# Batch 2's K and Q brought in and cast earlier, and the opening reordered, in a sliding-window attention and feed-forward kernel

## The chip, the cores and the metric

The kernel runs on one core of a Trainium2 chip. The time is device microseconds of one execution. Lower is better. The runs of the kernel before are summarised by their median.

## The reference

Eight batches of eight heads, 576 positions, head size 64. Each query sees itself and the 63 positions before it. The heads' outputs are put side by side and go through a feed-forward block with a product of two projections.

```python
scores = (1 / sqrt(64)) * q @ k.T
scores = where((rel >= 0) & (rel < 64), scores, -1e9)   # rel = query position - key position
attn   = softmax(scores)
x      = (attn @ v) as [8 * 576, 512]                   # heads side by side
out    = ((x @ w1) * (x @ w2)) @ w3 @ w_out             # w1, w2: 512x1024; w3: 1024x1024; w_out: 1024x512
```

All inputs and the output are float32.

## The kernel before

The kernel keeps everything in fp16 on the core and accumulates in fp32. Its order is written out by hand: each engine executes its instructions in the order in which the Python code issues them, and waits only for the data and buffers that the next instruction needs. TensorE is PE, VectorE is DVE, ScalarE is ACT, GpSimd is POOL, and SP only issues transfers.

*Attention.* A batch's K and Q come as float32 rows into a tile `stage` (three buffers, 1.18 MB each, two transfers for the even and the odd heads, L210). `cast_qk` (L226) turns each half into fp16 in `k16` or `q16`, of which there is one buffer each. `transposes` (L262, copies L266) turns them into `kT` and `qT`, 18 PE transposes in three groups of six, through banks of the accumulation memory. V normally arrives already in its place `v16` by transfers with a cast on the way (`load_v`, L241, issued by POOL); `copy_v` (L245) fills overlapping blocks on DVE. Batch 0's V is the exception: it comes as rows, is cast, transposed (`transposes(0, "v", ...)`) and transposed back by `keys_of_v` (L273, L275).

`scores(d)` (L296) makes the scores of one half of a third of a batch, so a batch has six: 0 to 5 are batch 0, 6 to 11 are batch 1. ACT takes the exponentials into `pt` (L300, six buffers), and POOL cuts the window out of it with two selects per piece (L308, L310). The scores share a single bank pair `s_ps`, so the next `scores` waits for the exponential of the last. `values(d)` multiplies by V (L338 in batches 0 and 1, L354 later), ACT forms the reciprocal of the sums as exp(-ln) (L344, L345; later L360 to L362), and DVE multiplies it into `xT` (L346; later L363, L364).

*Feed-forward.* `w3 @ w_out` is folded once into `wc_sb`: `fold_t(fc)` transposes one 128-row block of w3 (L492, copy L493) and `fold_mm(fc, half, ...)` multiplies it by half of w_out (L501, copy L503). For each group of 512 tokens `ffn_ab(g, fc)` makes one 128-wide chunk of both projections (16 matmuls, L432; copy by ACT L437; product by DVE L438), and `ffn_o(g, t)` makes 128 rows of output (8 matmuls L450, copy L452). `store` sends them off on SP (L459). The banks `f_ps` are three and are shared by folding and feed-forward.

*The stages.* The opening loads K and Q of batch 0 on SP, and POOL issues the transfers with a cast for weights and rows: w3 (`load_w3`, L482), w_out (`load_wo`, L476), rows (`load_rows`, L217), w1 and w2 in two halves of columns each (`load_w12`, L471; the second half serves chunks 4 to 7). Then batch 0's attention runs interleaved with the folding, and `keep_busy(n)` (L527) puts n matmuls on the identity, whose result nobody reads, between them. Then group 0 of the feed-forward runs with batch 1's attention: scores 6, 7, ... between `ffn_ab(0, ...)`, then the loop over d = 6 to 11, which issues `values(d)`, `scores(d + 3)` and one step of the feed-forward, and in its last three rounds the three groups of K transposes of batch 2. After that a general schedule of ticks handles batches 2 to 7.

Batch 2's K and Q are loaded by `load_qk` on SP. The one for K has a gate: a one-column memset on POOL into the tile, for which SP must wait, so the transfer cannot start before POOL reaches it. Batch 2's four casts stand on POOL, one in each of the rounds d = 6 to 9. SP handles its transfers strictly in order too: those for `lnsum` (sums kept for a range check, `keep_sums`, L369) stand between the loads and the stores.

Of the kernel before, what the change touches and what calls it, by code (L numbers as in the profile page):

```python
# [144 lines left out]
def kernel(  # L145
# [11 lines left out]
    nc = tc.nc  # L157
# [30 lines left out]
    pool_cp = nc.gpsimd.tensor_copy  # L188
    dve_cp = nc.vector.tensor_copy
# [11 lines left out]
    def big_rows(which, b, hh):  # L201

        return {"k": k, "q": q, "v": v}[which][b, hh:H:2].rearrange("j (p r) d -> p j (r d)", r=TI)

    def load_qk(b, which, gate=None):
        t = sb.tile([P, 2, TI * D], FP32, name="stage", bufs=3)
        if gate is not None:
            gate(t[:, 0, 0:1], 0.0)
        for hh in range(2):
            nc.sync.dma_start(out=t[:, hh], in_=big_rows(which, b, hh))  # L210
        raws[which, b] = t

    def load_rows(b, which):
# [11 lines left out]
    def cast_qk(b, which, hh, cp):  # L225
        cp(t16_of(b, which)[:, :, hh * D:hh * D + D], raws[which, b][:, hh].rearrange("p (i d) -> p i d", d=D))  # L226
# [8 lines left out]
    def load_v(b, *blocks):  # L235

        vh = v_heads(b)
        for c in blocks:
            lo = D if c == 4 else 0
            s0 = VBLK[c] + lo  # L240
            nc.gpsimd.dma_start(out=vh[lo:P, c], in_=v[b, :, s0:s0 + P - lo, :].rearrange("h s d -> s h d"))  # L241
# [10 lines left out]
    def transposes(b, which, *cs, into=None, cps=None):  # L252

        t16 = t16s[which, b]
        if cs[0] == 0:
            turned[which, b] = sb.tile([P, NJ, S], FP16, name=which + "T", bufs=1 if which == "v" else 2)
        dst = turned[which, b]
        if into is None:
            into = [ps_t.tile([P, 6, P], FP16, name="tp")]
        for c, tp in zip(cs, into):  # L260
            for i in range(6):
                nc.tensor.transpose(tp[:, i, :], t16[:, 6 * c + i, :], ident16)  # L262
        if cps is None:
            cps = [dve_cp if which == "k" or c != 1 else act_cp for c in cs]
        for c, tp, cp in zip(cs, into, cps):
            cp(dst.rearrange("q j (p i) -> q j p i", i=TI)[:, :, :, 6 * c:6 * c + 6],  # L266
               tp.rearrange("q i (p j) -> q j p i", p=TP))

    def keys_of_v(b, js, into, cps):

        for j, tp in zip(js, into):
            for c in range(6):
                nc.tensor.transpose(tp[:, c, :], turned["v", b][:, j, VBLK[c]:VBLK[c] + P], ident16)  # L273
        for j, tp, cp in zip(js, into, cps):
            cp(v16s[b % 2][:, :, j].rearrange("p c (a e) -> p c a e", a=2)[:, :, :, 0:D],  # L275
               tp.rearrange("p c (a e) -> p c a e", a=2))
# [5 lines left out]
    def scores(d):  # L282

        b, r = divmod(d, 6)
        si, jp = divmod(r, 2)
        kT, qT = turned["k", b], turned["q", b]
        seg = SEGS[si]
        w = sum(blk[2] for blk in seg)
        s_ps = ps_s.tile([P, 2, 2, 256], FP32, name="s_ps")
        for jj in range(2):  # L290
            j = 2 * jp + jj
            c0 = 0
            for (k0, q0, n, _) in seg:
                for a in range(2):
                    half = slice(a * D, a * D + D)
                    nc.tensor.matmul(s_ps[:, a, jj, c0:c0 + n], kT[half, j, k0:k0 + P], qT[half, j, q0:q0 + n],  # L296
                                     start=True, stop=True, skip_group_check=True)
                c0 += n
        pt = sb.tile([P, 2, 2, 256], FP16, name="pt", bufs=6)
        nc.scalar.activation(pt[:, :, :, 0:w], s_ps[:, :, :, 0:w], AF.Exp, bias=-SHIFT, scale=scale)  # L300

        rows = pt.rearrange("k a j n -> k (a j) n")
        for (lo, nb, n, off, step) in MASKS[si]:
            sl = rows[:, :, lo:lo + nb * n]
            pat = [[0, 4], [step, nb], [1, n]]
            if nb == 1:
                pat = [[0, 4], [1, n]]
            nc.gpsimd.affine_select(out=sl, in_=sl, pattern=pat, compare_op=ALU.is_ge,  # L308
                                    fill=0.0, base=off, channel_multiplier=-1)
            nc.gpsimd.affine_select(out=sl, in_=sl, pattern=[[-s, m] for s, m in pat], compare_op=ALU.is_ge,  # L310
                                    fill=0.0, base=63 - off, channel_multiplier=1)
        probs[d] = pt
# [161 lines left out]
    def load_wo(half):  # L474
        cols = slice(half * 256, half * 256 + 256)
        nc.gpsimd.dma_start(out=wo16[:, :, cols], in_=moe_w_out[:, cols].rearrange("(e p) m -> p e m", p=P))  # L476
# [10 lines left out]
    def fold_t(fc, cp=dve_cp):  # L487

        w3 = turned_w3(fc)
        tp = ps_f.tile([P, 8, P], FP16, name="f_ps")  # L490
        for ec in range(8):
            nc.tensor.transpose(tp[:, ec, :], w3[:, ec, :], ident16)  # L492
        cp(w3, tp)  # L493

    def fold_mm(fc, half, cp, nf=1):

        cols = slice(half * 256, half * 256 + 256)
        o_ps = ps_f.tile([P, 2, 256], FP32, name="f_ps")
        for f in range(nf):
            for ec in range(8):  # L500
                nc.tensor.matmul(o_ps[:, f], turned_w3(fc + f)[:, ec, :], wo16[:, ec, cols],  # L501
                                 start=(ec == 0), stop=(ec == 7), skip_group_check=True)
        cp(wc_sb[:, fc:fc + nf, cols], o_ps[:, 0:nf])  # L503
# [19 lines left out]
    def keep_busy(n):  # L523

        d = ps_t.tile([P, P], FP32, name="tp")
        for _ in range(n):
            nc.tensor.matmul(d, ident16, ident16, start=True, stop=True)  # L527


    load_qk(0, "k")  # L530
    load_qk(0, "q")
    nc.scalar.preload_act_table_set("natural_log_exp_and_others")
    make_identity(nc, ident16)

    def ones_of(i):
        nc.gpsimd.memset(v16s[i].rearrange("p c j (a e) -> p (c j a) e", a=2)[:, :, D:2 * D], 1.0)

    ones_of(0)
    ones_of(1)
    load_w3(0)  # L540
    load_wo(0)
    load_rows(0, "v")
    for n in range(1, 4):
        load_w3(n)
    load_wo(1)

    def bank(pool, name):

        t = pool.tile([P, 2, 1024] if name != "f_ps" else [P, 1, 1024], FP16, name=name)
        return t[:, 0, 0:768].rearrange("p (i n) -> p i n", i=6)  # L550

    def tp_bank():
        return ps_t.tile([P, 6, P], FP16, name="tp")

    def three():
        return [bank(ps_v, "o_ps"), tp_bank(), bank(ps_s, "s_ps")]
# [8 lines left out]
    transposes(0, "q", 0, 1, 2, into=three(), cps=[act_cp, dve_cp, act_cp])  # L565
    keep_busy(6)
    scores(0)
    keep_busy(6)
    fold_t(0)
    scores(1)  # L570
    fold_t(1)
    for i in range(2):
        load_w12(i, 0)
    scores(2)
    keep_busy(6)
    fold_mm(0, 0, dve_cp)
    scores(3)
    load_rows(1, "k")
    fold_mm(1, 0, dve_cp)
    scores(4)  # L580
    cast_qk(0, "v", 0, dve_cp)
    cast_qk(0, "v", 1, act_cp)
    keep_busy(6)
    transposes(0, "v", 0, 1, 2, into=[bank(ps_v, "o_ps"), tp_bank(), bank(ps_f, "f_ps")], cps=[dve_cp, act_cp, dve_cp])
    scores(5)
    load_rows(1, "q")
    for i in range(2):
        load_w12(i, 1)
    load_v(1, 0, 2, 3)
    fold_t(2)  # L590
    keys_of_v(0, [0, 1, 2], [bank(ps_v, "o_ps"), tp_bank(), bank(ps_f, "f_ps")], [act_cp, dve_cp, act_cp])
    fold_t(3)
    fold_mm(2, 0, act_cp)
    keys_of_v(0, [3], [tp_bank()], [dve_cp])
    fold_mm(3, 0, act_cp)
    fold_t(4)
    values(0)
    fold_t(5)
    fold_mm(4, 0, dve_cp)
    values(1, ps_s)  # L600
    fold_mm(5, 0, dve_cp)
    fold_t(6)
    values(2)
    fold_t(7)
    fold_mm(6, 0, dve_cp)
    values(3, ps_s)
    fold_mm(7, 0, dve_cp)
# [3 lines left out]
    fold_mm(2, 1, dve_cp, 2)  # L611
    fold_mm(4, 1, dve_cp, 2)
    load_v(1, 4, 5)
    fold_mm(6, 1, dve_cp, 2)
    cast_qk(1, "k", 0, dve_cp)
    cast_qk(1, "k", 1, act_cp)
# [5 lines left out]
    transposes(1, "k", 0, 1, 2, into=three(), cps=[dve_cp, act_cp, dve_cp])  # L622
    cast_qk(1, "q", 0, dve_cp)
    cast_qk(1, "q", 1, act_cp)
    ffn_ab(0, 1)
    ffn_ab(0, 2)
    transposes(1, "q", 0, 1, 2, into=three(), cps=[dve_cp, act_cp, dve_cp])
    ffn_ab(0, 3)
    scores(6)
    copy_v(1, 1)  # L630
    ffn_ab(0, 4)
    scores(7)
    load_qk(2, "k", nc.gpsimd.memset)
    load_qk(2, "q")
    ffn_ab(0, 5)
    scores(8)
    copy_v(1, 4)
    load_v(2, 0, 2, 3)
    steps = [lambda fc=fc: ffn_ab(0, fc) for fc in range(6, 8)] + [lambda t=t: ffn_o(0, t) for t in range(4)]
    for d in range(6, 12):  # L640
        values(d, ps_s if d in (9, 11) else None)
        if d < 9:
            scores(d + 3)
        steps.pop(0)()
        store()
        if d == 6:
            load_v(2, 4, 5)
            load_qk(3, "k")
        if d < 10:
            cast_qk(2, "kq"[(d - 6) // 2], d % 2, pool_cp)  # L650
        if d > 8:
            transposes(2, "k", d - 9)
    for hh in range(2):
# [73 lines left out]
```

## Time and profile before

| | |
|---|---|
| median of 9 runs | 299.2 us (296.62 to 299.4) |
| the profiled execution's own time | 297.91 us |
| its span, first to last instruction | 296.2 us |
| PE busy | 278.9 us (94%) |
| POOL busy | 178.9 us (60%) |
| DVE, ACT busy | 180.1 us, 168.0 us |
| bytes moved by transfers | 37.68 MB |

The span and every position below are microseconds from the first instruction. The matmuls' ends are modelled, so a PE that is shown busy can still be running slowly. PEclk is the clock that PE was granted, as a share of full speed.

### The profile page before, as it was taken

What the parts mean: (1) busy time and instruction counts of PE and PEld (TensorE: products, weight loads), DVE (VectorE), ACT (ScalarE), POOL (GpSimd) and SP (SyncE); (2) the same over time, 40 slices, a digit from 0 to 9 for tenths busy, and PEclk for the clock granted to TensorE, in tenths of its full rate; (3) what the DMA queues carried; (4) which work ended last, traced back from release to release, by engine and by line L of the source; (5) the groups of instructions that cost most, each with busy time, mean ns of one, the idle gap of its engine ahead of it and who ended that gap; (6) DMA issues with size and microseconds to landing.
All of it is one profiled execution on the core that took longest, in us unless ns stands there. A gap on an engine that the chain in (4) does not pass through costs nothing.

```text
span 296.2 us, 6258 instructions
## 1 busy us (share of the span) xinstructions
PE 278.9 (94%) x2433; PEld 163.3 (55%) x2433; DVE 180.1 (61%) x281; ACT 168.0 (57%) x276; POOL 178.9 (60%) x215
## 2 busy tenths in 40 slices
PE   7779899995989999999999999999999999999992
PEld 7658786442554545555555787555555444544441
DVE  0536646643486766868768766668767656545531
ACT  2666444682247647775776656397657866641310
POOL 8799820499459956598769553796695453411300
PEclk9999999998699999999999999999999999999998
DMA  6999999079776938295819480970096021002003
GB/s 238 231 211 204 210 200 62 3 255 308 106 254 265 73 80 276 118 62 128 320 40 105 134 308 0 108 118 2 1 151 76 0 74 72 2 35 108 2 37 112
DMA packets 48449, 37.68 MB, mean 127 GB/s; under 512 B 34160, under 2 KB 38512, under 8 KB 48416
## 3 DMA queue, kind: packets, MB, share of 16 engines
q0 software_dynamic: 38960, 11.14, 37.6%
q1 hardware_dynamic: 9312, 25.97, 24.4%
q8 instruction: 20, 0.33, 0.5%
q10 hardware_dynamic: 144, 0.13, 0.1%
q14 instruction: 13, 0.11, 0.1%
HBM read 38.80 MB, written 9.44 MB: 163 GB/s over the span
## 4 chain that ended last, share of the span: by engine, by line
PE 87%; ACT 4%; DVE 4%; POOL 2%; issue 1%; POOLq 0%; DVEq 0%; ACTq 0%
PE f_ps L432 41%; PE f_ps L450 21%; PE tp L262 5%; PE o_ps L354 5%; PE s_ps L296 5%; PE f_ps L501 4%; PE tp L527 3%; PE o_ps L338 1%; ACT pt L300 1%; POOL k L226 1%; PE f_ps L492 1%; DVE xT L346 1%; DVE vT L266 1%; ACT r L345 1%; ACT q L229 1%
## 5 line engine op out<-in xcount | busy, mean ns | idle before, releaser
L432 PE MATMUL f_ps<-xT,w_sb 128*128 128x512 f16 (+1 forms) x640 | 134.2, 358 | 0.0
L308 POOL TENSOR_SCALAR_AFFINE_SELECT pt<-pt 128x512 f16<-128x512 f16 (+1 forms) x64 | 52.2, 815 | 72.8 <-ACT pt L300 72.8
L432 PEld LDWEIGHTS <-w_sb 128*128 128x128 f16 x640 | 59.7, 98 | 50.4 <-issue 0.3
L450 PE MATMUL f_ps<-wc_sb,ab 128*128 128x512 f16 (+1 forms) x296 | 68.7, 380 | 0.1
L438 DVE TENSOR_TENSOR ab<-f_ps,a_sb 128x512 f16<-128x512 f32 x72 | 49.8, 692 | 22.1 <-PE f_ps L432 18.0
L437 ACT COPY a_sb<-f_ps 128x512 f32<-128x512 f32 x72 | 41.7, 579 | 28.7 <-PE f_ps L432 27.9
L300 ACT ACTIVATE pt<-s_ps 128x1024 f16<-128x1024 f32 (+1 forms) x48 | 45.7, 951 | 20.9 <-PE s_ps L296 19.4
L310 POOL TENSOR_SCALAR_AFFINE_SELECT pt<-pt 128x512 f16<-128x512 f16 (+1 forms) x64 | 51.8, 810 | 4.5
L363 DVE TENSOR_TENSOR xT<-o_ps,r 64x384 f16<-64x384 f32 x36 | 19.8, 550 | 39.4 <-ACT r L362 39.4
L450 PEld LDWEIGHTS <-ab 128*128 128x128 f16 x296 | 27.8, 99 | 28.9 <-issue 2.2
L360 ACT ACTIVATE ln_s<-o_ps 64x384 f32<-64x384 f32 x36 | 17.5, 487 | 32.4 <-PE o_ps L354 32.4
L452 DVE COPY t2k<-f_ps 128x512 f32<-128x512 f32 (+1 forms) x36 | 24.5, 683 | 13.9 <-PE f_ps L450 13.4
L241 POOL DMA_DIRECT2D v<-in_v_dram x35 | 29.6, 853 | 2.1 <-DMA rows<-in_k_dram 1.1
L354 PEld LDWEIGHTS <-v 128*128 128x128 f16 x288 | 18.1, 98 | 8.7 <-ACT pt L300 0.8
L354 PE MATMUL o_ps<-pt,v 128*128 128x128 f16 (+1 forms) x288 | 20.7, 215 | 0.4 <-DVE xT L364 0.4
L296 PEld LDWEIGHTS <-kT 64*128 64x128 f16 x384 | 10.7, 94 | 17.7 <-issue 16.1
L364 DVE TENSOR_TENSOR xT<-o_ps,r 64x384 f16<-64x384 f32 x36 | 20.2, 561 | 0.5
L362 ACT ACTIVATE r<-ln_s 128x384 f32<-128x384 f32 x36 | 18.8, 522 | 1.1
L296 PE MATMUL s_ps<-qT,kT 64*128 64x128 f16 (+1 forms) x384 | 18.2, 214 | 1.2 <-ACT pt L300 1.1
L266 DVE COPY kT<-tp 128x768 f16<-128x768 f16 x18 | 17.1, 952 | 3.4 <-PE tp L262 3.3
L361 ACT ACTIVATE ln_s<-o_ps 64x384 f32<-64x384 f32 x36 | 17.4, 482 | 0.4
L226 POOL CAST k<-stage 128x1152 f16<-128x1152 f32 x12 | 13.7, 1149 | 4.5 <-PE tp L262 4.5
(88 smaller groups left out, 236.6 us busy)
## 6 DMA issues: line engine op xcount, KB each, us to landing
out_dram<-t2k SPq DMA_DIRECT2D x35, 256.0 KB
stage<-in_k_dram SPq DMA_DIRECT2D x14, 576.0 KB
stage<-in_q_dram SPq DMA_DIRECT2D x14, 576.0 KB
v<-in_v_dram POOLq DMA_DIRECT2D x28, 128.0 KB, 4.6
w_sb<-in_moe_w_dram POOLq DMA_DIRECT2D x4, 512.0 KB, 12.4
ab<-in_moe_w_dram POOLq DMA_DIRECT2D x2, 512.0 KB, 8.5
ab<-in_moe_w_out_dram POOLq DMA_DIRECT2D x2, 512.0 KB, 12.7
xT<-in_moe_w_dram POOLq DMA_DIRECT2D x2, 512.0 KB, 14.3
```

Of the source, the lines that this page charges most:

```text
L241: nc.gpsimd.dma_start(out=vh[lo:P, c], in_=v[b, :, s0:s0 + P - lo, :].rearrange("h s d -> s h d"))
L296: nc.tensor.matmul(s_ps[:, a, jj, c0:c0 + n], kT[half, j, k0:k0 + P], qT[half, j, q0:q0 + n], start=True, stop=True, skip_group_check=True)
L300: nc.scalar.activation(pt[:, :, :, 0:w], s_ps[:, :, :, 0:w], AF.Exp, bias=-SHIFT, scale=scale)
L308: nc.gpsimd.affine_select(out=sl, in_=sl, pattern=pat, compare_op=ALU.is_ge, fill=0.0, base=off, channel_multiplier=-1)
L310: nc.gpsimd.affine_select(out=sl, in_=sl, pattern=[[-s, m] for s, m in pat], compare_op=ALU.is_ge, fill=0.0, base=63 - off, channel_multip ...
L354: nc.tensor.matmul(o_ps[:, jj, o0:o0 + n], v16[:, si * 2 + bi, j0 + jj, a * D:a * D + P], pt[:, a, jj, c0:c0 + n], start=first, stop=(bi = ...
L364: nc.vector.tensor_tensor(xs[D:P], o_ps[D:P, :, 192:384], r[D:P], ALU.mult)
L432: nc.tensor.matmul(d[:, f * n + c0:f * n + c1], w[:, dc, (fc + f) * P:(fc + f + 1) * P], xT[:, dc, xc:xc + c1 - c0], start=first, stop=(dc ...
L437: act_cp(a_sb[:, 0:nf * n], a_ps[:, 0:nf * n])
L438: nc.vector.tensor_tensor(ab[:, fc:fc + nf, lo:hi], b_ps[:, 0:nf * n].rearrange("p (f n) -> p f n", f=nf), a_sb[:, 0:nf * n].rearrange("p ...
L450: nc.tensor.matmul(o_ps[:, 0:c1 - c0], ab[:, fc, t * P:t * P + P], wc_sb[:, fc, c0:c1], start=(fc == 0), stop=(fc == 7))
L452: cp(o_sb[:, c0:c1], o_ps[:, 0:c1 - c0])
```

## The change

1. The first loads: the even heads of K and Q of batch 0 stay on SP, the odd heads' two transfers go to ACT's queue. On POOL the memset of ones into the second V buffer (`ones_of(1)`) moves from ahead of the weight transfers to behind them.
2. The opening: `keep_busy` goes from 6, 6, 6 to 4, 0, 10 around scores 0, 2 and 4 (the last of the three stood ahead of the V transposes). Both halves of batch 0's V are cast on DVE, ahead of scores 4; before, one half was cast on ACT behind it. One V copy goes from DVE to ACT, one `keys_of_v` copy from ACT to DVE, two `fold_mm` copies from DVE to ACT. Each `fold_t` from the third on is issued two steps ahead of its `fold_mm`.
3. Batch 1: Q's transposes come one `ffn_ab` earlier, and so do scores 6, 7, ...: the loop issues `scores(d + 4)`.
4. Batch 2: K and Q are issued right behind `load_v(1, 4, 5)`, K's gate on POOL with them. K's two casts on POOL stand ahead of the selects of scores 6, Q's two ahead of those of scores 8. Batch 3's K load is issued before the loop and no longer in round d = 6.

```diff
-    def load_qk(b, which, gate=None):
+    def load_qk(b, which, gate=None, other=None):
...
-            nc.sync.dma_start(out=t[:, hh], in_=big_rows(which, b, hh))
+            (other if hh and other else nc.sync).dma_start(out=t[:, hh], in_=big_rows(which, b, hh))
...
-    load_qk(0, "k")
-    load_qk(0, "q")
+    load_qk(0, "k", other=nc.scalar)
+    load_qk(0, "q", other=nc.scalar)
...
     ones_of(0)
-    ones_of(1)
     load_w3(0)
...
     load_wo(1)
+    ones_of(1)
...
     scores(0)
-    keep_busy(6)
+    keep_busy(4)
     fold_t(0)
...
     scores(2)
-    keep_busy(6)
     fold_mm(0, 0, dve_cp)
     scores(3)
     load_rows(1, "k")
     fold_mm(1, 0, dve_cp)
+    for hh in range(2):
+        cast_qk(0, "v", hh, dve_cp)
     scores(4)
-    cast_qk(0, "v", 0, dve_cp)
-    cast_qk(0, "v", 1, act_cp)
-    keep_busy(6)
-    transposes(0, "v", 0, 1, 2, into=[bank(ps_v, "o_ps"), tp_bank(), bank(ps_f, "f_ps")], cps=[dve_cp, act_cp, dve_cp])
+    keep_busy(10)
+    transposes(0, "v", 0, 1, 2, into=[bank(ps_v, "o_ps"), tp_bank(), bank(ps_f, "f_ps")], cps=[dve_cp, act_cp, act_cp])
+    fold_t(2)
+    fold_t(3)
     scores(5)
...
-    fold_t(2)
-    keys_of_v(0, [0, 1, 2], [bank(ps_v, "o_ps"), tp_bank(), bank(ps_f, "f_ps")], [act_cp, dve_cp, act_cp])
-    fold_t(3)
+    keys_of_v(0, [0, 1, 2], [bank(ps_v, "o_ps"), tp_bank(), bank(ps_f, "f_ps")], [act_cp, dve_cp, dve_cp])
     fold_mm(2, 0, act_cp)
     keys_of_v(0, [3], [tp_bank()], [dve_cp])
+    fold_t(4)
     fold_mm(3, 0, act_cp)
-    fold_t(4)
+    fold_t(5)
     values(0)
-    fold_t(5)
-    fold_mm(4, 0, dve_cp)
+    fold_mm(4, 0, act_cp)
+    fold_t(6)
     values(1, ps_s)
-    fold_mm(5, 0, dve_cp)
-    fold_t(6)
+    fold_mm(5, 0, act_cp)
+    fold_t(7)
     values(2)
-    fold_t(7)
...
     load_v(1, 4, 5)
+    load_qk(2, "k", nc.gpsimd.memset)
+    load_qk(2, "q")
...
     cast_qk(1, "q", 1, act_cp)
+    for hh in range(2):
+        cast_qk(2, "k", hh, pool_cp)
     ffn_ab(0, 1)
+    transposes(1, "q", 0, 1, 2, into=three(), cps=[dve_cp, act_cp, dve_cp])
     ffn_ab(0, 2)
-    transposes(1, "q", 0, 1, 2, into=three(), cps=[dve_cp, act_cp, dve_cp])
+    scores(6)
     ffn_ab(0, 3)
-    scores(6)
+    scores(7)
     copy_v(1, 1)
+    for hh in range(2):
+        cast_qk(2, "q", hh, pool_cp)
     ffn_ab(0, 4)
-    scores(7)
-    load_qk(2, "k", nc.gpsimd.memset)
-    load_qk(2, "q")
-    ffn_ab(0, 5)
     scores(8)
     copy_v(1, 4)
     load_v(2, 0, 2, 3)
+    ffn_ab(0, 5)
+    scores(9)
+    load_qk(3, "k")
...
-        if d < 9:
-            scores(d + 3)
+        if d < 8:
+            scores(d + 4)
         steps.pop(0)()
         store()
         if d == 6:
             load_v(2, 4, 5)
-            load_qk(3, "k")
-        if d < 10:
-            cast_qk(2, "kq"[(d - 6) // 2], d % 2, pool_cp)
```

## The prediction

> **What bounds the kernel now.** I read the page first: which engine fills the span, and where it doesn't. The rows are 40 slices of 7.4 us.
>
> ```profile
> PE   7779899995989999999999999999999999999992
> PEclk9999999998699999999999999999999999999998
> ```
>
> PE is full from slice 12 on, so what can be gained lies in the first 84 us, and in the opening and in slices 8 to 10 above all, where the clock falls too. The waits name what PE waited for (total us, times, longest):
>
> ```profile
> PE tp L262 <- POOL k L226: 3.2, 1, 3.2
> PE o_ps L262 <- ACT k L226: 1.7, 1, 1.7
> ```
>
> The chain that ended last shows the first of them (start, us, what):
>
> ```profile
> 68.43 1.15 POOL k L226
> 69.58 1.06 POOL pt L308
> 70.70 1.09 POOL pt L310
> 71.80 1.10 POOL k L226
> 72.94 0.82 PE tp L262 x6
> 73.77 0.99 PE o_ps L338 x13
> 74.76 3.53 PE f_ps L450 x8
> ```
>
> Batch 2's K casts hold up its transposes: PE stops at 69.73 and starts at 72.94. The windows show the clock (us; busy PE, PEld, DVE, ACT, POOL; PEclk; DMA share; GB/s):
>
> ```profile
> 40.00:48.00 8.00, 8.00 (x75) 6.40 (x74) 4.07 (x7) 2.90 (x5) 0.00 (x0) 1.00 2.23 162
> ...
> 72.00:73.00 1.00, 0.06 (x1) 0.06 (x2) 0.00 (x0) 0.00 (x0) 1.00 (x2) 0.61 1.57 279
> ...
> 78.00:79.00 1.00, 1.00 (x11) 0.72 (x11) 0.68 (x2) 0.00 (x0) 0.00 (x0) 0.50 0.00 0
> 79.00:80.00 1.00, 1.00 (x19) 0.67 (x18) 0.92 (x2) 0.39 (x1) 0.00 (x0) 0.98 0.12 45
> ```
>
> PE works on at half speed until 79. POOL did nothing from 40 to 55, but in that stretch the transfers were still busy. The timeline shows the second wait:
>
> ```profile
> 19.55 0.70 DVE L226 COPY k<-rows 128x1152 f16<-128x1152 f16 x1
> ...
> 20.67 1.14 ACT L226 COPY k<-rows 128x1152 f16<-128x1152 f16 x1
> ...
> 21.87 0.51 PE L262 MATMUL o_ps<-ident,k 128*128 128x128 f16 x6 [1.71 <-ACT k L226]
> ```
>
> **Batch 2's casts (gain 5.0).** Removed: the wait of 3.2 and the slow pieces. The chain's six transposes, values, `ffn_o`, six transposes and values took 0.82 + 0.99 + 3.53 + 0.64 + 0.64 = 6.6; the same pieces at full clock take 0.50 + 0.49 + 1.85 + 0.44 + 0.57 = 3.85. So 2.8 more, 6.0 together. The Trainium skill, "TensorE: Matmul & The Clock Gate" ("Why this matters for your kernels"; Part 1), warns of PE gaps over about 3 us and has the full rate back after about 3.4 us of work. By that the slow clock cost 3.4 / 2 = 1.7 and my total would be 1.1 less. Here half speed lasted six microseconds after PE restarted, so I take 2.8. The same rule speaks against thinning `keep_busy`; the trace's longest gap in the opening, 20.15 to 21.87, left PEclk at 1.00, and the new order makes it shorter. Cost 0; if a gap there did reach 3 us, another 2.8.
>
> What is paid back: Q's transposes of batch 1 now follow `ffn_ab(0,1)`, which ends at 49.4 by the old clock. The Q casts end at 49.39 (ACT) and 49.72 (DVE); with K's casts on POOL beside it the DVE cast is nearer 0.70 than 0.45 (both lengths are in the trace, the long one beside a busy POOL). PE waits 0.6, and scores 6 start at T = 52.85 instead of 53.95. The wait of scores 9 for the bank (0.7) becomes one of scores 10.
>
> POOL from T on: first exponential, ready at T + 1.3; selects of scores 6 and 7, 2.2 each; Q casts 2.25; selects 8, 2.25; three V issues 2.65; selects 9 and 10, 4.5; two V issues 1.6; selects 11, 2.25. That ends at T + 21.2. PE up to `values(11)`: five `ffn_ab` 9.15, three `ffn_o` 5.55, six scores 1.9, five values 2.7, two groups of transposes 0.9, the wait 0.7, so T + 20.9. PE waits 0.3 to 0.4 there; `values(9)` (PE at T + 15.2, POOL at T + 15.05) just passes. 6.0 - 0.6 - 0.4 = 5.0, bounds 4.0 and 5.6. Batch 3's K casts still wait for batch 2's last K transposes (one `k16`), so they move with them. K's own casts must be done by T + 1.3; see the transfers.
>
> **The opening (gain 2.0).** PE's idle time between 19 and 36 sums to 3.1 in windows of 1 us: 1.7 ahead of the V transposes, 0.4 ahead of `keys_of_v`, 0.8 at L501 behind late `fold_t` copies, the rest scattered. New: scores 4 still wait for the exponential of scores 3 and end at 19.6. DVE casts both V halves from 19.5 to 20.9 (2 x 0.70, behind the `fold_mm` copy), the ten `keep_busy` (0.085 each) fit into that wait, and V's transposes start at 20.95 instead of 21.87: 0.9. The V copies end on ACT at 23.5 (0.96 on DVE; 0.81 + 0.81 on ACT), the two `fold_t` fill that time, `keys_of_v` starts at 23.6, and `fold_mm(2)` at 24.6 instead of 25.83 with the same work behind it: 1.2. With `fold_t` two steps ahead the waits of 0.44 and 0.34 at L501 (31.33, 35.72) go too: 2.0 to 2.2. The weights were there: the last w3 block had landed by 26.5 (issue 10.9, longest landing 15.6), and its `fold_t(6)` is now due at 29.2. Bounds: 0.9 (the cast alone) and 2.2; I take 2.0. The `fold_mm` copies moved to ACT (0.37 each) lie between its exponentials; ACT was busy 3.2 of 8 us there. The fewer `keep_busy` at scores 0 and 2 are worth at most 0.1, since the next scores wait for ACT.
>
> **The first loads (0).** `keep_busy(75)` holds PE until 8.64, and K was cast by 7.9. An earlier K changes nothing. Two more issues on ACT, 0.65 each, delay its table load, which was done at 2.2 and is first needed at 6.67. POOL issues the weights 2.6 earlier (half of the two memsets' 5.25), while Q still loads. Q was there before its first cast at 10.06. Bounds: 0, and a loss of 0.6 if the weights take a third of the rate. I take 0. The moved memset ends at 12.9, ahead of the first select at 14.93.
>
> **The transfers (loss 0.6).** K and Q of batch 2 are gated by a memset behind `load_v(1,4,5)`, whose last issue began at 38.72 after a wait for an earlier transfer. So they go at about 39.5. On SP they now stand ahead of three `lnsum` (nobody waits for those soon), and batch 3's K follows at 43.5, ungated, where it used to follow at 62.39. That is 3 x 1.18 MB, 8.4 us at the 420 GB/s of the first loads, laid upon POOL's backlog, which drained until 48.5:
>
> ```profile
> 7.00:8.00 1.00, 1.00 (x18) 1.00 (x16) 0.91 (x2) 0.50 (x1) 1.00 (x2) 1.00 1.04 424
> 8.00:9.00 1.00, 1.00 (x22) 1.00 (x20) 0.00 (x0) 0.00 (x0) 1.00 (x3) 1.00 1.11 370
> 9.00:10.00 1.00, 1.00 (x22) 1.00 (x19) 0.98 (x2) 0.65 (x1) 1.00 (x3) 1.00 1.03 179
> ...
> v<-in_v_dram POOLq DMA_DIRECT2D x7, 128.0 KB, 10.4
> ```
>
> Who yields? The first windows sum to 2.38 MB by 9.0, just SP's loads, though POOL had issued from 6.60: POOL's queue got next to nothing beside SP's. The last row, transfers issued between 55 and 100, says the same: V took 10.4 from issue to landing beside K and Q, against 4.6 over the whole run. The skill's "DMA: Bandwidth & Descriptors" ("Queues, rings and completion order") has each DMA engine take the queues in turn, packet by packet. By the rule the weights keep a share and cost nothing. By the rows everything of POOL's moves back by 8.4: the second half of w1 and w2, landed by 46.8 at the latest (32.6 + 14.2), would come at 55.2, w2 last, and `ffn_ab(0,4)` wants w2 at 54.1 (T less the opening's 2.0, plus 2.4, plus half of the 1.83 for w1): a wait of 1.1. V of batch 1 would land by 56.9; `copy_v(1,4)` wants it near 56 and holds only DVE's product of chunk 5, due at 57. I take 0.6, bounds 0 and 1.6 (V's wait added). K2 itself lands by 46 to 48, its casts are done by 50, and selects 6 come at 52: covered by two microseconds.
>
> **Sum.** 5.0 + 2.0 + 0 - 0.6 = 6.4. The profiled execution took 297.91 (span 296.2 and 1.7 around it) and would take 291.5. It lies 1.3 under the median of 299.2; the median becomes 292.8. From 81 us on I expect no change: PE is full, the order is the same.
>
> **The rivals.**
> *POOL becomes the bound* (chance 0.17). Its 19.9 us of work from scores 6 to 11 have no slack. Against it: only the Q casts are new there, and two K casts leave. If the selects or V issues start or run 2 to 4 us later in all, values 9 and 11 wait as long, and half the gain goes: 295.5.
> *The loads are not early* (0.06). If the gate opens late, or K2 lands ten microseconds after issue as V did, its casts end past 56 and selects 6 with them; the K stall is traded for one at `values(6)`: about 298.
> *Starved weights* (0.07, slower). If the transfers hold back w1 and w2's second half by x beyond need at `ffn_ab(0,4)`, PE stands still for x, and past about 2.7 us (when the clock fell in the trace) loses another 2.8. The gain before this is 7.0. It decides from x = 4.2 on, w2 at 58.3; with x = 6 the time is 299.2 - 7.0 + 8.8 = 301. Against it: conservation of bytes gives x of 1.1 at full starvation.
> *A little more* (0.04): all bounds good, 7.8: 291.4 or under.
>
> **How the numbers follow.** The likeliest case, 292.8, has 0.66 and runs from 291.4 to 294.6. Reaching into the POOL rival, and 0.6 below for a median's scatter, gives 290.8 to 296.8. A difference of 0.5%, 1.5 us, is about what a measurement of this kernel can tell from none. Faster by more: 0.66 + 0.04 + 0.16 + 0.01 = 0.87; within: 0.06; slower: 0.07.
>
> **What would show it.** Right: no wait of PE for POOL's K cast, PEclk 1.00 from 64 to 84, first `ffn_ab` near 43 instead of 45.1, K2's casts between 45 and 50, wait of `values(11)` under 1 us. Wrong: a wait of L432 for `w_sb`, `copy_v` waiting for V over 1 us, POOL's selects of scores 6 starting after 53, or PEclk under 1 anywhere before 84.

## The result and the profile after

The changed kernel takes 293.78 us (median of 10 runs, 291.47 to 298.24) against 298.02 for the kernel before, measured anew (median of 31): ratio 0.9876 [0.9841, 0.9912], so 3.7 us by the ratio, 4.2 by the medians. Measured again (run 5), the ratio was 0.9877 [0.9836, 0.9918]. The forecast was 292.8, with 291.4 to 294.6 for the likeliest case, and a gain of 6.4. The time lies in that range, but the gain is only about six tenths of the forecast one. That the range held is in part luck: the kernel before was itself 1.2 us quicker than the 299.2 from which the forecast started, and from 299.2 the measured ratio leads to 295.5. The profiled execution took 292.94 (span 291.1) and lies 4.97 under the profiled one of before. So there are two questions. In the traces 1.4 us of the gain are missing; and the median gained about one microsecond less than the traces.

Lay the two traces side by side at events that both have (us from the span's start):

| event | before | after | after is earlier by |
|---|---|---|---|
| scores 0 | 13.66 | 14.88 | -1.22 |
| V transposes | 21.87 | 22.47 | -0.60 |
| `keys_of_v` | 24.39 | 24.93 | -0.54 |
| first `ffn_ab` | 44.94 | 44.14 | 0.80 |
| Q transposes of batch 1 | 51.12 | 49.96 | 1.16 |
| scores 6 | 53.95 | 52.78 | 1.17 |
| third K transposes of batch 2 | 81.23 | 76.36 | 4.87 |
| end | 296.2 | 291.1 | 5.1 |

The whole gain is there by 76 us, as forecast, but the change *lost* 1.22 us before the first scores, where the forecast had nothing. The same two rows of the page as before:

```profile
PE   7589998989899999999999999999999999999992
PEclk9999999999999999999999999999999999999998
```

Slices 8 to 10, counted from 0, hold 8 or more and the clock stays at full rate, but slice 1, from 7.3 to 14.6 us, now holds 5. PE's waits up to 90 us (total us, times, longest) say for what:

```profile
PE f_ps L262 <- DVE k L229: 1.7, 1, 1.7
PE tp L527 <- POOL ident masks.py:199: 1.5, 1, 1.5
PE s_ps L296 <- ACT pt L300: 1.4, 2, 1.1
PE s_ps L262 <- DVE q L229: 1.3, 1, 1.3
PE o_ps L262 <- DVE q L226: 1.2, 1, 1.2
PE o_ps L262 <- DVE k L226: 1.0, 1, 1.0
...
PE s_ps L338 <- POOL pt L310: 0.2, 1, 0.2
```

The 3.2 for POOL's K cast is gone. In its place stand four waits for *DVE's* casts: of K and Q in the opening (1.7 and 1.3), of Q of batch 1 (1.2) and of V (1.0). The timeline shows the first two (start, us, engine, line, operation):

```profile
5.85 1.11 POOL L217 DMA_DIRECT2D rows<-in_v_dram  x2
6.83 3.57 DVE L229 CAST k<-stage 128x768 f16<-128x768 f32 x2 [6.83 <-DMA stage<-in_k_dram]
6.92 0.75 POOL L482 DMA_DIRECT2D ab<-in_moe_w_dram  x1
7.62 1.49 POOL L482 DMA_DIRECT2D xT<-in_moe_w_dram  x2
9.05 0.96 POOL L476 DMA_DIRECT2D ab<-in_moe_w_out_dram  x1
9.95 3.05 POOL L536 MEMSET v<- 128x3072 f16 x1
10.46 0.51 PE L262 MATMUL f_ps<-ident,k 128*128 128x128 f16 x6 [1.69 <-DVE k L229]
12.05 1.36 DVE L229 CAST q<-stage 128x768 f16<-128x768 f32 x1
```

Two K casts take 3.57 us on DVE. The lengths one by one (min, median and max in ns) show that this is not a general slowness:

```profile
L229 DVE CAST k<-stage x2: 561/1828/3095, 6.8 to 7.3; 128x768 f16<-128x768 f32 x2
```

The first took 0.56 as in before; the second began at 7.3 and ended at 10.40, 0.4 after the last of POOL's issues. In before the two took 0.56 and 0.75, and Q's 0.61. Q's now starts beside POOL's memset and ends 0.4 after it (12.05 + 1.36 = 13.41; 9.95 + 3.05 = 13.0). Nothing else is late there: K landed at 6.83, ACT's casts beside them took 0.83 as before, and DVE's two copies out of the banks, from 10.32 on beside the memset, took 1.80 together (1.82 before). In before POOL was issuing beside DVE's casts as well. Its chain of issues had only just begun when K's casts came; Q's cast stood in the middle of it:

```profile
6.60 0.95 POOL L482 DMA_DIRECT2D ab<-in_moe_w_dram  x1
...
6.68 1.22 DVE L229 CAST k<-stage 128x768 f16<-128x768 f32 x2 [6.68 <-DMA stage<-in_k_dram]
7.55 0.91 POOL L476 DMA_DIRECT2D ab<-in_moe_w_out_dram  x1
...
10.21 1.49 POOL L482 DMA_DIRECT2D xT<-in_moe_w_dram  x2
10.75 0.61 DVE L229 CAST q<-stage 128x768 f16<-128x768 f32 x1
```

In the stretch of batch 2, the answer to before's chain (start, us, what) is

```profile
58.62 2.24 POOL q L226 x2
60.86 1.06 POOL pt L308
...
63.08 2.60 POOL v L241 x3
65.68 1.13 POOL pt L308
...
70.19 1.53 POOL v L241 x2
71.71 1.12 POOL pt L308
72.91 1.11 POOL pt L310
74.06 0.64 PE s_ps L338 x16
```

POOL carries the chain from 54.1 to 74, as the rival had it, and yet PE waits only 0.2 for it: the two run neck and neck. The transfers, by windows (us; busy PE, PEld, DVE, ACT, POOL; PEclk; DMA share; GB/s) and by issues (KB each, median us from issue to landing, issues before 50 us):

```profile
7.00:8.00 1.00, 1.00 (x22) 1.00 (x20) 1.00 (x2) 0.65 (x1) 1.00 (x2) 1.00 1.04 429
9.00:10.00 1.00, 0.00 (x0) 0.00 (x0) 1.00 (x1) 0.78 (x2) 1.00 (x3) 1.00 1.15 216
40.00:48.00 8.00, 8.00 (x72) 6.04 (x70) 4.86 (x8) 2.94 (x5) 0.74 (x1) 1.00 1.26 303
```

```profile
w_sb<-in_moe_w_dram POOLq DMA_DIRECT2D x4, 512.0 KB, 11.1
...
v<-in_v_dram POOLq DMA_DIRECT2D x4, 128.0 KB, 19.7
```

PE has no busy time at all from 9 to 10 us: that is the wait for K. Between 40 and 48 the core moved 303 GB/s instead of 162. V's landing went from 13.1 us in before to 19.7. But w1 and w2, issued by 34.0 and landing in 12.0 at most, were there at 46.0, nine microseconds before `ffn_ab(0,4)`, which began at 55.17.

### The profile page after: what moved, and what is told of

It reads as the page before. It is cut to its first block, busy times and chain, and to the rows that moved or that the text cites. A ratio compares the mean times of both kernels' runs of the same rounds, so it can differ in the third digit from the quotient of the medians.

```text
span 291.1 us, 6248 instructions
## 1 busy us (share of the span) xinstructions
PE 275.4 (95%) x2429; PEld 161.6 (55%) x2429; DVE 183.9 (63%) x280; ACT 167.8 (58%) x277; POOL 180.0 (62%) x215
## 4 chain that ended last, share of the span: by engine, by line
PE 80%; POOL 7%; DVE 6%; ACT 2%; DMA 2%; issue 1%; DVEq 0%; POOLq 0%; SPq 0%; ACTq 0%
PE f_ps L432 38%; PE f_ps L450 20%; PE o_ps L354 5%; PE tp L262 5%; PE f_ps L501 5%; PE s_ps L296 4%; POOL pt L310 2%; POOL pt L308 2%; DMA stage<-in_k_dram 2%; DVE kT L266 1%; POOL v L241 1%; DVE k L229 1%; ACT pt L300 1%; PE f_ps L492 1%; PE s_ps L338 1%
## 5 line engine op out<-in xcount | busy, mean ns | idle before, releaser
L450 PE MATMUL f_ps<-wc_sb,ab 128*128 128x512 f16 (+1 forms) x296 | 67.0, 373 | 0.1
```

What stands on the lines that cost most here:

```text
L450: nc.tensor.matmul(o_ps[:, 0:c1 - c0], ab[:, fc, t * P:t * P + P], wc_sb[:, fc, c0:c1], start=(fc == 0), stop=(fc == 7))
```

## The experiments

Three questions were put. Why did DVE's casts take 3.1 and 1.36 us? *Theory A*: DVE stands still while POOL works, and moving POOL's work ahead put it beside the casts. *Theory B*: loads on two queues slow the casts, since more transfers write beside them. Is the rest of the sum right, part by part? And why is the median's gain smaller than the trace's? *Clock theory*: PE's new idle time in the opening lets its clock fall in some runs.

Every edit is against the changed kernel unless it says otherwise, and every ratio is to the kernel before on the same chip, with its 95% interval. Runs 1 to 4 shared one chip, 5 to 8 another, 9 to 11 a third; the last had one of its own.

**1. The memset put back ahead of the weight loads** (POOL in the old order)

```
     ones_of(0)
+    ones_of(1)
     load_w3(0)
...
     load_wo(1)
-    ones_of(1)
```

> The changed kernel, with the second V buffer's memset of ones back ahead of POOL's weight transfers, so that POOL issues them from 6.6 us and not from 4.0. In the changed kernel DVE's second cast of K took 3.1 us and that of Q 1.36, where they took 0.56 to 0.75 and 0.61 before. Theory A (a DVE cast from one on-chip tile to another stands still while POOL writes descriptors or memsets): both casts come back under 0.8, scores 0 start near 13.7 instead of 14.88, and the whole is 1.0 to 1.3 us shorter than the changed kernel. Theory B (K's rows coming in faster on two queues, together with POOL's weights, slow the casts): the casts stay above 1.5, since the loads are still on two queues. Theory C (the opening lost its time elsewhere): casts come back, first feed-forward matmul stays at 44.1.

Measured: 291.82 us (290.46 to 294.23), 0.9772 [0.972, 0.9824]. The casts were back to their length and scores 0 at 13.44 instead of 14.88. By its lines for L229 (ns):

```profile
L229 DVE CAST k<-stage x2: 560/600/641, 6.8 to 7.3; 128x768 f16<-128x768 f32 x2
L229 DVE CAST q<-stage x1: 550/550/550, 10.1 to 10.1; 128x768 f16<-128x768 f32 x1
```

The changed kernel's own ratio is from other chips, so the comparison by time is left to run 6. One line of POOL moved gives 1.44 us back ahead of scores 0. That speaks for A: the loads still ran on two queues. In this trace most of it was lost again by the first `ffn_ab` (43.96 against 44.14), since PE's clock was at half from 12.8 to 16.2 and the wait for V's cast was 1.5 instead of 1.0:

```profile
13.00:14.00 1.00, 1.00 (x15) 0.66 (x14) 0.00 (x0) 0.02 (x1) 0.00 (x0) 0.50 1.39 182
...
16.00:17.00 1.00, 0.89 (x15) 0.70 (x14) 0.46 (x2) 0.62 (x1) 0.93 (x3) 0.88 1.15 218
```

**2. Both halves of the first loads on SP again** (POOL in the new order)

```
-    load_qk(0, "k", other=nc.scalar)
-    load_qk(0, "q", other=nc.scalar)
+    load_qk(0, "k")
+    load_qk(0, "q")
```

> The changed kernel, with the first loads of K and Q all on SP again, POOL's order as changed (weights from 4.0 us). Theory A (POOL's work blocks DVE's casts): the second K cast stays at 2.5 to 3.2 us, scores 0 stay at 14.9 or a little later since K lands later or at the same time; the whole within 0.5 us of the changed kernel. Theory B (two queues of loads slow the casts): the cast falls back to 0.6 to 0.8 and scores 0 come at 13.7.

Measured: 292.58 us (292.41 to 295.62), 0.9804 [0.9771, 0.9837]. With one queue the casts were not quicker. In its trace, which is of its slowest run, *both* K casts stood:

```profile
7.12 6.29 DVE L229 CAST k<-stage 128x768 f16<-128x768 f32 x2 [7.12 <-DMA stage<-in_k_dram]
...
9.95 3.04 POOL L536 MEMSET v<- 128x3072 f16 x1
...
13.46 0.34 PEld L262 LDWEIGHTS <-k 128*128 128x128 f16 x6 [2.33 <-DVE k L229]
```

The first ended at 10.40 behind POOL's last issue, the second at 13.4 behind the memset; scores 0 came at 17.93. Theory B falls: the casts stood with one queue too. The other six runs are 1.7 to 3.2 us shorter, which would fit one cast fewer held up, but no trace of them shows it. That the ratio is no worse than the changed kernel's was not expected. By time alone runs 1 and 2 cannot be told apart, for their intervals overlap; the lengths of the casts tell them apart.

**3. K's casts of batch 2 held until Q's casts of batch 1 are done** (a copy of one column on POOL, which reads Q's cast)

```
+    held = const.tile([P, 1], FP16)
+    pool_cp(held, t16_of(1, "q")[:, 0, 0:1])
     for hh in range(2):
         cast_qk(2, "k", hh, pool_cp)
```

> The changed kernel, with one more POOL instruction ahead of batch 2's K casts: a copy of one column of batch 1's cast Q, for which POOL must wait until DVE's Q cast is done. In the changed kernel that cast took 1.34 us (0.45 before) beside POOL's K casts, and PE waited 1.2 us for it. Theory A (POOL's casts block DVE's): the Q cast takes 0.45, PE's wait falls to 0.2 to 0.4, K's casts run from about 49 to 51.3, still ahead of the selects of scores 6; gain 0.8 to 1.0 us over the changed kernel. Rival (the Q cast waits for its transfer or for DVE's copies): no change of the wait, 0 us or a small loss.

Measured: 292.35 us (289.91 to 293.04), 0.9787 [0.9754, 0.982]. The Q cast that had taken 1.34 beside POOL's K casts took

```profile
L226 DVE COPY q<-rows x1: 450/450/450, 46.8 to 46.8; 128x1152 f16<-128x1152 f16 x1
```

and PE's wait of 1.2 for it became one of 0.3 for ACT. One trace would not show that the edit did it, since this cast was sometimes short without it too (0.57 in run 5, 0.45 in run 9). But with the edit it took 0.45 in all four traces (runs 3, 6, 8, 12), and without it, with K's casts of batch 2 on POOL beside it, 1.33 to 1.39 in six of eight. So A holds at a second place, with casts on POOL in the issues' stead. In run 3's trace the opening's K casts happened to escape as well (0.56 both; Q's took 1.04), so its span of 288.1 is not the edit's alone.

**4. Batch 2's part alone**, behind the opening of before

```
-    load_qk(0, "k", other=nc.scalar)
...
+    load_qk(0, "k")
...
+    ones_of(1)
     load_w3(0)
...
-    fold_t(2)
-    fold_t(3)
     scores(5)
...
```

> The changed kernel's treatment of batches 1 and 2 (parts 3 and 4) behind the opening of the kernel before (parts 1 and 2 undone). My ledger of the two traces gives parts 3 and 4 4.1 us and the opening 0.8: so 4.0 to 4.4 us under the kernel before, feed-forward starting at 45.1, no wait for a K cast, PEclk 1.00 from 64 to 90. If the opening had given its 2.0 and parts 3 and 4 only 3.1: 3 us. If the transfers laid upon POOL's backlog bite: a wait for w1 or w2 at the chunks 4 and later.

Measured: 294.2 us (293.21 to 296.06), 0.9841 [0.9805, 0.9877]: 4.7 us, where the forecast had 5.0. No wait for POOL's K cast is left, `values(11)` waits 0.5, and DVE's Q cast takes 1.34 here too. Its trace had a clock that stood at half from 11.6 to 18.4, after a wait of 2.3 for ACT's Q cast:

```profile
12.00:13.00 1.00, 0.96 (x10) 0.96 (x11) 0.10 (x1) 0.75 (x1) 0.76 (x1) 0.50 1.38 183
...
17.00:18.00 1.00, 1.00 (x14) 0.77 (x8) 0.48 (x1) 0.77 (x1) 0.93 (x3) 0.50 1.15 214
```

**5. The changed kernel again**, in one comparison with the next three

> The changed kernel itself, unchanged, on the same chip as the next three, as their yardstick and for a second trace of it. If its early POOL issues make DVE's casts a matter of luck (Theory A with a race): the casts of K may be 0.56 or about 3 this time, the ratio stays near 0.988, and the runs spread over 4 us. If the first trace showed a fixed cost: the same 3.1 us cast again. Either way I expect mean clocks between 0.987 and 0.999, since the PE clock fell in the opening in three of the five other traces (from 12 to 18 us).

Measured: 294.69 us (291.79 to 295.09), 0.9877 [0.9836, 0.9918]. The long casts came again (K 0.65 and 3.13, Q 1.36), with scores 0 at 14.86. The Q cast of batch 1 took 0.57 this time, and its trace's span was 290.1 at a mean clock of 1.000; the runs at 294.6 to 295.1 had 0.985 to 0.986.

**6. Edits 1 and 3 together**

> The changed kernel with both mends: the memset of ones back ahead of POOL's weight transfers, and batch 2's K casts held until DVE's cast of Q of batch 1 is done. Theory A (POOL's work blocks DVE's casts): the two gains add, no DVE cast of K or Q above 0.8 us, 1.5 to 2.5 us under the changed kernel. Rival (what is won in the opening is lost at the next wait, for the weights behind batch 2's loads): about the gain of one mend alone, and a PE wait at chunk 4 or later for w1 or w2.

Measured: 290.66 us (290.03 to 291.63), 0.9745 [0.9705, 0.9786]. Beside run 5 on the same chip that is 4.0 us, and the intervals do not overlap. Not all of it is the casts' own time. The two traces are 1.2 us apart (spans 288.9 and 290.1), and the one run of run 5 at a full clock (291.79) is 0.9 to 1.8 above run 6's five at 0.996 to 0.999. The rest goes with the clock, which was lower in most of run 5; whether the held-up casts caused that is not shown. K's casts took 0.55 and 0.56, both Q casts 0.55 and 0.45. Scores 0 came at 13.37, the first `ffn_ab` at 42.63, scores 6 at 50.39: the forecast for the change itself had "near 43" and 50.85. PE still waits 1.0 for DVE's V cast of 1.41.

**7. The opening alone** (new loads, POOL's new order, V's casts and `fold_t`), with batch 2 as before

```
     load_v(1, 4, 5)
-    load_qk(2, "k", nc.gpsimd.memset)
-    load_qk(2, "q")
...
-    for hh in range(2):
-        cast_qk(2, "k", hh, pool_cp)
     ffn_ab(0, 1)
...
```

> Parts 1 and 2 of the change alone (first loads on two queues, memset behind the transfers, the reordered opening), batches 1 and 2 as in the kernel before. Parts 3 and 4 alone gave a ratio of 0.9841, 4.7 us, and the whole change 0.9876. If the parts add up: the opening alone is between 1.0 us slower and 1.5 us faster than before, with the stall of 3.2 us for the K cast and the half clock still there. If the opening was worth the 2.0 of my prediction: ratio 0.993 and the first feed-forward matmul at 43.

Measured: 297.21 us (293.81 to 300.81), 0.9972 [0.9934, 1.001]: by the interval between 2.0 us quicker and 0.3 slower, so not told from no change. The casts took 0.69 and 3.13 (K) and 1.36 (Q), the first `ffn_ab` came at 44.13, and POOL's K cast cost PE its 3.2 again. The half clock around that wait's end lasted 3.4 us here (72.2 to 75.6), against 6.8 in before (72.2 to 79.0):

```profile
73.00:74.00 1.00, 1.00 (x17) 0.83 (x18) 0.96 (x1) 0.00 (x1) 0.93 (x2) 0.50 2.40 159
...
76.00:77.00 1.00, 1.00 (x13) 0.61 (x13) 0.32 (x1) 0.00 (x0) 0.51 (x1) 1.00 0.35 22
```

**8. Run 6 with more `keep_busy` between K's and Q's first transposes**

```
-    keep_busy(10)
+    keep_busy(22)
```

> The kernel with both mends, and 22 instead of 10 of the unused identity matmuls between K's and Q's transposes, about 1 us of PE in the wait for Q's casts. In three of six traces PE's clock fell to one half between 12 and 18 us, after PE had stood idle for 0.4 to 2 us in the stretch from 9 to 13. Clock theory: with that idle time filled no run shows it, all mean clocks are 0.995 or more, and the median is 1 to 2 us under the one with both mends alone. Rival (the clock falls for another reason, or the matmuls only push the transposes back): mean clocks spread as before, median the same or 0.2 to 0.5 us more.

Measured: 291.01 us (290.13 to 292.54), 0.9774 [0.9733, 0.9815]; clocks 0.990 to 0.997 against 0.992 to 0.999 in run 6. A miss: filling that idle time raised neither the clock nor the speed.

**9. ACT takes the casts from DVE** (POOL still in the new order)

```
-        cast_third(0, "k", c, act_cp if c == 1 else dve_cp)
+        cast_third(0, "k", c, act_cp if c >= 1 else dve_cp)
...
-        cast_third(0, "q", c, dve_cp if c == 2 else act_cp)
-    transposes(0, "q", 0, 1, 2, into=three(), cps=[act_cp, dve_cp, act_cp])
+        cast_third(0, "q", c, act_cp)
+    transposes(0, "q", 0, 1, 2, into=three(), cps=[dve_cp, dve_cp, act_cp])
```

> The changed kernel with POOL's early order kept, but only the first third of K cast on DVE: the third one and all of Q on ACT, two of Q's copies on DVE in return. Theory A (a DVE cast stands still beside POOL's descriptor writing): ACT's casts take 0.83 each and never more, K is ready by 8.6 or 9, scores 0 come at 13.8 to 14.2 instead of 14.88, and the PE clock falls less often; 1 to 3 us under the changed kernel (ratio 0.977 to 0.984). Rival (the rows were not all there, or the transfers slow every reader): ACT's casts are long too, above 1.5, ratio 0.988.

Measured: 292.64 us (290.63 to 294.52), 0.9839 [0.9797, 0.9881]. Beside the same issues and the same memset ACT's casts kept their length:

```profile
L229 ACT CAST q<-stage x3: 830/834/835, 9.7 to 11.1; 128x768 f16<-128x768 f32 x3
L229 ACT CAST k<-stage x2: 827/832/836, 6.6 to 7.4; 128x768 f16<-128x768 f32 x2
```

and scores 0 came at 13.43, the first `ffn_ab` at 42.70. It is DVE beside POOL that stands, not any cast beside transfers. The median improves less than the trace (span 288.9): the two runs at a mean clock of 0.988 took 294.2 and 294.5, those at 0.996 took 290.6 and 290.7.

**10. The changed kernel with PE's wait for K filled by `keep_busy(20)`**

```
-    transposes(0, "k", 0, 1, 2, into=[bank(ps_f, "f_ps") for _ in range(3)], cps=[dve_cp, act_cp, dve_cp])
+    transposes(0, "k", 0, 1, into=[bank(ps_f, "f_ps") for _ in range(2)], cps=[dve_cp, act_cp])
+    keep_busy(20)
+    transposes(0, "k", 2, into=[bank(ps_f, "f_ps")], cps=[dve_cp])
```

> The changed kernel with 20 more unused identity matmuls between the second and the third group of K's transposes, where PE waited 1.5 to 1.7 us for the blocked cast. The casts stay as they are (about 3.1). Four of six runs of the changed kernel on the last chip had a mean clock of 0.985 or 0.986 and took 294.6 to 295.1, the one at 1.000 took 291.8. Clock theory (the wait for the blocked cast lets the PE clock fall): mean clocks 0.994 and more in all runs, median 291.5 to 292.5, scores 0 still near 14.9. Rival (the clock falls on account of something else): clocks spread from 0.985 to 1.000 as before, ratio 0.988.

Measured: 293.37 us (292.44 to 293.78), 0.9851 [0.9822, 0.988]. The long cast stays (3.13), scores 0 stay at 14.86, only PE's idle time is filled (its wait is 0.3). The clocks of all six runs were 0.994 to 1.000, where four of six were at 0.985 to 0.986 in run 5 (on another chip): that agrees with the clock theory. But the median missed what was expected of it, and the interval overlaps with the changed kernel's. The theory is not shown.

**11. The changed kernel, one more trace**, to catch a fallen clock

> The changed kernel once more, unchanged, for a third trace of it: in two runs out of three its PE clock fell somewhere, and neither of its two traces so far shows where. If the clock falls: at half speed for 3 to 6 us beginning between 11 and 14, right behind the wait for the blocked K cast. A fall anywhere else (52 to 62, or 76 to 79) would speak against that.

Measured: 292.6 us in one run, clock 1.000. The casts were long again (K 3.13, Q 1.36, Q of batch 1 1.33), but the clock did not fall. Where it falls in the changed kernel's slower runs was never seen in a trace.

**12. Run 6 with V's second cast on ACT**, beside DVE's first

```
-    for hh in range(2):
-        cast_qk(0, "v", hh, dve_cp)
+    cast_qk(0, "v", 0, dve_cp)
+    cast_qk(0, "v", 1, act_cp)
...
-    transposes(0, "v", 0, 1, 2, into=[bank(ps_v, "o_ps"), tp_bank(), bank(ps_f, "f_ps")], cps=[dve_cp, act_cp, act_cp])
+    transposes(0, "v", 0, 1, 2, into=[bank(ps_v, "o_ps"), tp_bank(), bank(ps_f, "f_ps")], cps=[dve_cp, act_cp, dve_cp])
```

> The kernel with both mends, and batch 0's V cast half on DVE and half on ACT again, ahead of scores 4 (one V copy back on DVE). On DVE alone the second half took 1.41 us in every trace with it there, beside POOL's issues for w1 and w2, and PE waited 1.0 us for it. Theory A (POOL's issues block DVE, never ACT): ACT's cast takes 1.14, from about 18.9 to 20.0; V's transposes come at 20.1 instead of 20.97, the first feed-forward matmul 0.5 to 0.9 us earlier than 42.63, ratio 0.971 to 0.974. Rival (ACT's exponentials, pushed back by 0.7, then hold up scores 5 and the values): transposes early, first feed-forward matmul at 42.6 all the same, ratio as for both mends, 0.9745.

Measured: 289.65 us (289.03 to 290.49), 0.9727 [0.9686, 0.9767], 8.1 us under before. It is the lowest ratio of all, but its interval overlaps with run 6's. V's casts took 0.45 (DVE) and 1.14 (ACT), its transposes started at 19.78 and the first `ffn_ab` at 41.49. A new wait stands in the way now, by the waits of PE and of DVE:

```profile
PE o_ps L338 <- DVE v L247: 1.1, 1, 1.1
```

```profile
DVE v L245 <- DMA v<-in_v_dram: 2.8, 1, 2.8
```

V of batch 1 lands 21.8 us after its issue (34.48 to 56.28), behind batch 2's loads: the wait for V that the forecast had within its bounds for the transfers. It appears only once PE is early enough to need V before it lands. About half of the 1.1 is DVE beside POOL again: the copy of V (L247) then took 1.00 beside POOL's Q casts, where the changed kernel's took 0.39.

## Where the prediction held and where it was off, step by step

**The first loads, priced at 0: the step that failed.** It asked what the earlier issues do to the *transfers* ("a loss of 0.6 if the weights take a third of the rate"). That did not happen: K and Q landed in time. What moved with the memset was POOL's chain of eight issues, from 6.60–12.6 to 4.0–10.0: it was in full course when K's casts began, and the memset behind it now ran beside Q's. The step named the memset's new end (12.9; measured 13.0) and asked only who needs its result, not what DVE does beside it. Cost: 1.22 us at scores 0.

The traces sort by POOL's order. With the new order and two K casts on DVE, one or both stood for 3.1 us or more in six of seven traces (not in run 3). With the old order none of six did; the longest took 0.83. Moving POOL's line back cured it (run 1), taking DVE out of it cured it (run 9), undoing the queues did not (run 2). The Trainium skill, "SBUF — State Buffer" ("Who interferes with whom"), has a mechanism: DVE and GpSimd share a pair of ports as an exclusive lock, which DVE needs in some of its modes (a cast can run in one), whoever issues first has it for the whole instruction and the other blocks, while PE and ACT wait for no one. The traces agree on the block and on ACT (0.83 throughout), and POOL paid at times as well: in run 3, where K's casts passed, the two issues of V's rows beside them took 1.40 instead of 1.11. But "the whole instruction" is too low a price here: the K cast began at 7.3 and got through only after four issues in a row, 3.1 us where the longest single one lasted under 1. The lock itself is not seen in a trace, nor is it shown which mode the casts ran in.

One thing stays open. In before K's casts and Q's ran beside POOL's issues too, and took 0.56 to 0.75. So standing beside POOL's issues is not enough to hold up a cast, and what decides whether one is caught was not found. What is shown is that POOL's order and the choice of DVE together made the loss. The forecast had two durations of a cast of 128x1152 in hand, "the long one beside a busy POOL", and used the long one for V of batch 0 and Q of batch 1, not for the first casts.

**The opening, 2.0: right in itself.** From scores 0 to the first `ffn_ab` it took 31.28 us before and 29.26 after, a gain of 2.02. The V casts were too cheap at 2 x 0.70: the two took 1.78 from 20.64, beside POOL's issues for w1 and w2. So V's transposes gained 0.6 instead of 0.9, `fold_mm(2)` 1.1 instead of 1.2, and what follows it 0.9 where the forecast had about 0.8: that the total fits to 0.02 is in part luck. The sum failed ahead of this step, not in it. Run 7 shows it from outside: the opening as a whole is worth no measurable time, for most of what it gains it first loses.

**Batch 2's casts, 5.0: right mechanism, two terms too small.** The wait of 3.2 and the slow pieces went, K's casts ran from 47.26 to 49.50, and alone the part gave 4.7 (run 4). Inside it the wait for batch 1's Q cast was 1.2, not 0.6, since the cast took 1.34, not "nearer 0.70": again DVE beside POOL's casts, undone by run 3. The wait for a bank of scores 10 was 1.1, not 0.7, and `values(11)` waited 0.2, not 0.4. The 2.8 for the half clock were what before's trace had, where it lasted 6.8 us. Run 7's 3.4 us at half rate cost about 1.7 by the same reckoning, the figure that the forecast had weighed and set aside. PE worked all through run 7's 3.4 us; in before it stood for 0.7 of the first 3.4, and the half clock went on for as long again. (It fell at 72.2 in before, 2.5 us after PE stopped, not about 2.7 as the rival of the starved weights has it.)

**The transfers, -0.6: did not come.** The weights' second half had landed by 46.0, not 55.2. The forecast let POOL's queue stand while SP's loads run, as in the first 9 us. Here it was otherwise: SP issued K and Q from 39.17, but the windows from 40 on (as above) show no more than POOL's backlog had drawn, until 43:

```profile
42.00:43.00 1.00, 1.00 (x12) 0.90 (x10) 0.41 (x1) 0.00 (x0) 0.00 (x0) 1.00 1.42 177
43.00:44.00 1.00, 1.00 (x11) 0.90 (x10) 0.29 (x1) 0.00 (x0) 0.00 (x0) 1.00 1.60 311
```

So the backlog seems to have gone on first. V did yield (its first transfer, issued at 34.8, was there at about 54.5), which cost PE nothing in this kernel and part of the 1.1 us in run 12.

**The sum.** 6.4 less 1.2 (casts in the opening), 0.6 (Q cast) and 0.4 (bank), plus 0.6 (transfers) and 0.2 (`values(11)`), is 5.0, against 4.97 between the profiled executions.

**The signs and the rivals.** Of the signs of "right", all but one came: no wait for POOL's K cast, PEclk 1.00 from 64 to 84, K2's casts in time, `values(11)` under 1 us. The first `ffn_ab` came at 44.1 instead of "near 43". Of those of "wrong" one came: selects of scores 6 at 54.11, after 53. They were late not for want of K2, but because scores 6 themselves were: 52.78, and the exponential 1.3 behind, as forecast. POOL is the bound on the chain as the first rival said, but at a price of 0.2. The loads were early, and no weight was starved.

**The median.** The changed kernel's fast runs go with the mean clock: 291.5 to 292.9 at 0.996 to 0.999, 292.4 to 295.7 below that. The trace of after had 0.997 and lies 0.84 under its median; that of before had 0.985, in the middle of before's runs, and lies 0.11 under its own. So the traces flatter the change. Five of the 14 traces show the clock at half for a stretch ahead of the span's end, and each stretch was 3.4 us long (runs 1, 2 and 7) or 6.8 (before and run 4). What these five have in common is not one long wait but how little PE worked: in the 3.4 us ahead of the fall it was busy for 0.2 to 1.6 of them. In eight of the nine traces without a fall PE was busy for at least 1.7 in every stretch of that length from 8 us on to 250; the three of the changed kernel come down to 1.7. A low stretch did not always bring a fall (run 3 has one of 1.35, run 4 a second one of 1.56). So this is a pattern in a few traces, not a cause that was tested: filling PE's idle time went with a higher clock in run 10, on another chip, and not in run 8. What sets the fall off stays open.

## What to carry to other kernels

Before POOL's work is moved (a memset, casts, and the issuing of transfers, too), look in the timeline at what DVE casts or copies between tiles on the core beside its new place, and take the rest of POOL's chain there, not the cast's own length, as the upper bound of its price. Give it to ACT, hold POOL back with a tiny copy that reads the cast's result, or leave POOL where it was: in this kernel two such edits gave 4.0 us in the median, 1.2 of them between the traces. And a transfer that arrives later costs nothing until everything ahead of its use is quicker, so look at it again after each gain.

## What the runs showed of the hardware

- A DVE cast of 128x768 from float32 took 0.54 to 0.83 us where it was not held up and up to 3.3 where it was caught beside a chain of POOL's issues or a memset; whether none, one or both of two casts were caught varied from trace to trace. ACT's casts of the same size took 0.83 beside the same chain (run 9).
- Which queue yields is not fixed: at 7 to 9 us SP's loads took nearly all of the rate, at 39 to 43 POOL's backlog seems to have kept it (177 to 222 GB/s, then 311 and more).
- After one and the same stall of 3.2 us, the half clock lasted 6.8 us in one trace and 3.4 in another. The five half-clock stretches on record were all of one of these two lengths, and ahead of each PE had been busy for at most 1.6 of 3.4 us.
- The mean clock of one kernel varied from 0.985 to 1.000 between runs, with about 3 us between 291.79 and 294.6 to 295.1 on one chip.
